# Another first step (ScalarE takes level five, GpSimd part of u, later weight loads), and in the second step scalings and products ahead of weight conversions

## The chip, the cores and the metric

The kernel runs on 1 core of one Trainium2 chip. The metric is device time in microseconds (us). PE is TensorE (PEld its weight loads), DVE is VectorE, ACT is ScalarE, POOL is GpSimd, SP is SyncE, which issues most DMAs. All data are float32; an L and a number is a line of the kernel before.

## The reference, cut to what matters

Two blocks in a row. The first is a recurrence over 768 tokens for 4 x 8 heads of size 48; the second a dense layer with an activation on 3072 tokens.

```python
for t in range(S):                       # per batch and head, state is 48 x 48
    y[t] = r[t] @ (state + outer(u * k[t], v[t]))
    state = w[t][:, None] * state + outer(k[t], v[t])
x = y, with the heads side by side       # 3072 x 384
h = x @ w_in                             # 384 x 2048
out = (h * erf(softplus(h))) @ w_out     # 2048 x 384
```

## The kernel before, in words

The tokens are worked in twelve steps, `s` = 0 to 11, each 128 tokens of two batches. "First step" below is s = 0 (`attend_first`), "second step" is s = 1 (`attend`). The order of the instructions on all five engines is the order in which the program writes them (a manual schedule); each engine works through its own list and waits on semaphores.

**Inside a step.** The recurrence is solved by halving: `own` holds the products of r and k of each pair of tokens in blocks of 64 tokens. It is filled in six levels. At each level PE multiplies r and k (`level_products`, L691) into one of two PSUM banks, DVE multiplies r and k by products of w (`scale`, L357 in the first step by halves, L364 later, the "scalings"), and the result is copied from the bank into `own`: at level 1 by a product with a mask (L947 in the first step, L1087 later), at levels 2 to 5 by DVE's predicated copy with a mask (`take_level`, L701), at level 6 by two ACT copies (L708). The products of w (`tot_sb`) are made by GpSimd (L386 in steps 0 and 1, L438 later). For level 1, r and k with u multiplied in are kept apart in `rk1` (`prepare`, `multiply_u`): in the second step ACT makes both halves (L416, L419). After level 6 PE multiplies `own` by v into the PSUM tile `y` (L723, in two parts), k is transposed (L989 in the first step, L1116 later) and copied to `kT`, the state products follow (L798), a state for the middle of the step is copied out (`middle`), and r times the states is added to `y` (L749). ACT copies `y` out as `y3` and `xT` (L757, L770, L778); in the first step PE does part of that in between ("the hop", L764). `keep_busy` (L1043) and `stay_warm` (L1034) are PE products that nothing reads.

**Beside it, in the second step,** the dense layer of the step before begins: PE multiplies `xT` by w_in (L1206), in six blocks between the levels, two afterwards. w_in and w_out come as 64-bit numbers and are converted on the chip in 16 tiles, two rows of 128 features each: tiles 0 to 7 are w_in, and block n of the products needs tile n. The stages of one tile are named by letters: `l` loads the words (L181; three buffers), `b` scales the high words on ACT (L289), for tiles 0 and 1 into the PSUM tiles `m`, for the others into `y`; `r` scales the low words on ACT (L297) into `rest`; `h` shifts on DVE (L306) from `m` or `y` into the weight; `o` adds `rest` on GpSimd (L319). Since `y` is one tile, the high words of tile n + 1 wait for the shift of tile n, and the products of `own` and v wait for the shift of tile 7.

A load is held back by a small copy into its buffer (L211, L272, L274) from the value that it is to come after; SP issues loads in the written order. `wait_for` (L942) and a copy at L1080 do the same for GpSimd's queue: a one-column copy from the array that DVE's scaling writes, so that what follows on GpSimd comes after it.

In the first step the loads stand as: r, k of the first half, u, r and k of the second half, w, masks (all on SP); tile 0's words; r and k of the second step; v; tile 1's words; w of the second step; tile 2's words; v of the second step. In the second step's loop the shift of the next tile stands ahead of the scaling at levels 3 and up:

```python
if s == 1 and 2 < level:
    stages["h"](level + 1)
scale(s, level)
if s == 1 and level == 2:
    turns.pop("pending")()
if s == 1 and level < 3:
    stages["h"](level + 1)
```

with the addition (`o`) behind it on GpSimd, after the one-column copy of L1080.

Of the kernel before, what the change touches and what calls it, by code (L numbers as in the profile page):

```python
# [23 lines left out]
NJ = 2  # L24
# [67 lines left out]
def kernel(  # L92
# [71 lines left out]
    def products(shape, n=None):  # L164

        if n is None:
            n = turns["next"]
            turns["next"] = 1 - n
        names = "abc"[: len(shape) - 1]
        return banks[n][:].rearrange(  # L170
            f"p ({' '.join(names)}) -> p {' '.join(names)}", **dict(zip(names, shape[1:]))
        )
# [14 lines left out]
    def load_first():  # L187
        t = ins.tile([P, 2, JP, C], FP32, name="in")
        vt = ins.tile([P, NH, D], FP32, name="v")
        ws[0] = ins.tile([P, JP, C], FP32, name="w")  # L190
        n = JP // NJ
        b0, b1 = slice(0, n), slice(n, JP)
        turns["first"] = t5 = t[:].rearrange("p x n t -> p (x n t)").rearrange(
            "p (j x n t) -> p j x n t", j=NJ, x=2, n=NP
        )
        nc.sync.dma_start(out=t5[:, 0], in_=rkw[0][:, 0:2, b0])
        nc.sync.dma_start(out=u_sb[:], in_=u)
        nc.sync.dma_start(out=t5[:, 1, 0], in_=rkw[0][:, 0, b1])
        nc.sync.dma_start(out=t5[:, 1, 1], in_=rkw[0][:, 1, b1])
        nc.sync.dma_start(out=ws[0][:, b0], in_=rkw[0][:, 2, b0])  # L200
        nc.sync.dma_start(out=ws[0][:, b1], in_=rkw[0][:, 2, b1])
        nc.sync.dma_start(out=mask_sb[:], in_=masks)
        loaded[0] = t, vt
# [16 lines left out]
    def load_v(s):  # L220

        vt = loaded[s][1]
        nc.sync.dma_start(out=vt[:], in_=v[s])
# [113 lines left out]
    def rows(e, n=D):  # L337
        return slice(e * EP, e * EP + n)
# [51 lines left out]
    def prepare(s):  # L390


        if s < DIRECT:
            in_t = loaded[s][0]
            rk1 = att.tile([P, 2, JP, C], FP32, name="rk1", bufs=1)
            ready[s] = (rk1,)
            parts = 1 if s else NJ
            def multiply_u(i, x):
                n = slice(i * JP // parts, (i + 1) * JP // parts)
                with_u, plain = (  # L400
                    [
                        t.rearrange("p n (t two) -> p n t two", two=2)[..., one]
                        for t in (rk1[:, x, n], in_t[:, x, n] if s else turns["first"][:, i, x])
                    ]
                    for one in (x, 1 - x)
                )
                if not s and not (x and not i):
                    nc.vector.tensor_mul(
                        with_u[0], with_u[1],
                        u_sb[:, :, None].to_broadcast([P, NP, C // 2]),  # L410
                    )
                    nc.vector.tensor_copy(out=plain[0], in_=plain[1])
                    return
                for p in range(NP):
                    of = slice(p, None, NP)
                    nc.scalar.mul(  # L416
                        out=with_u[0][:, of], in_=with_u[1][:, of], mul=u_sb[:, p : p + 1]
                    )
                nc.scalar.copy(plain[0], plain[1])  # L419

            if s < 2:
                for i in range(parts):
                    for x in range(2):
                        multiply_u(i, x)
                return
            yield
            yield
            multiply_u(0, 0)
# [246 lines left out]
    def first_pair(x, n):  # L675

        return turns["first"][:, n // NP, x, n % NP]
# [19 lines left out]
    def take_level(own, pp, level):  # L697
        half = 1 << (level - 1)
        got = pp[:].rearrange("p e n t -> p (e n) t")
        if level <= MASKED:  # L700
            nc.vector.copy_predicated(  # L701
                rights(own[:], half),
                rights(mask_sb[:, level - 1 : level, :].to_broadcast([P, NH, HC]), half),
                got[..., : HC // 2].rearrange("p n (b h) -> p n b h", h=half),
            )
        else:
            for s0 in range(0, C, HC):
                nc.scalar.copy(own[s0 : s0 + half, :, half:], got[s0 : s0 + half, :, :half])  # L708
# [2 lines left out]

    def from_own(s, own, swap):
        vt = loaded[s][1]
        for j in range(NJ):
            for q in range(0, NP, 2):
                for h in range(NC):
                    e = h ^ swap
                    for p in (q, q + 1):  # L720
                        n = j * NP + p
                        t = slice(h * HC, (h + 1) * HC)
                        nc.tensor.matmul(  # L723
                            y[at(e, p), e, p // 2, j, t],
                            lhsT=vt[t, n * NE + e, :], rhs=own[t, e * JP + n, :],
                            start=swap == 1 and not j and not q, stop=True,
                            skip_group_check=True,
                        )
# [190 lines left out]
    def attend_first(xT):  # L919
# [32 lines left out]
        for level in range(2, LOG):  # L952
            pp = turns.pop("pp", None) or products([P, NE, JP, HC])
            for j, half in enumerate(halves):
                level_products(pp, first_pair, level, half)
                scale(0, level, batch=j)
            turns["pp"] = products([P, NE, JP, HC])
            keep_busy(turns["pp"], (DM,))
            take_level(own, pp, level)
            wait_for(1 << level - 1)  # L960
            if level == 2:
                totals(2, part=slice(batch // 2, batch))
            else:
                totals(*behind[level])
            if level == 2:
                stages["b"](0, 0)
                stages["b"](0, 1)
                stages["r"](0)
                for _ in prepare(1):
                    pass  # L970
                nc.sync.dma_start(out=vt[:], in_=v[0])
                stages["l"](1, own[:, 0, 2:3])
                nc.sync.dma_start(out=ws[1][:], in_=rkw[1][:, 2])
        totals = plan_totals(1)
        pp = turns.pop("pp")
        for j, half in enumerate(halves):
            level_products(pp, first_pair, LOG, half)
            scale(0, LOG, batch=j)
        take_level(own, pp, LOG)

        kT = att.tile([P, NH, D], FP32, name="kT", bufs=1)
        kT_by_e = kT[:].rearrange("p (e n) d -> p e n d", e=NE)
        turned = [products([P, NE, JP, HC])]
        keep_busy(turned[0], (DM,))
        for j, half in enumerate(halves):
            if j:
                turned.append(products([P, NE, JP, HC]))
            for i, n in enumerate(half):
                nc.tensor.transpose(  # L989
                    turned[j][:, 0, 2 * i : 2 * i + 2], first_pair(1, n), ident[:]  # L990
                )
        from_own(0, own, 1)
        for half, ps, copy in zip(halves, turned, (nc.scalar.copy, nc.vector.tensor_copy)):
            copy(
                kT_by_e[:, :, half.start : half.stop],
                ps[:, 0].rearrange("p (n e) d -> p e n d", e=NE)[..., :D],
            )
        stages["b"](1, 0)
        stages["b"](1, 1)
        fence()  # L1000
        stages["l"](2, seen[:, 0:1])
        load_v(1)
        stages["h"](0)
        stages["h"](0)
        ps = [[products([P, NE, JP, HC], 1 - e)[:, e] for e in range(NE)]]
        state_part(0, kT, ps, (0,))
        from_own(0, own, 0)
        nc.scalar.copy(middle[rows(1)], ps[0][1][rows(1), :, :D])
        nc.vector.tensor_copy(middle[rows(0)], ps[0][0][rows(0), :, :D])
        stages["r"](1)  # L1010
        stages["h"](1)
        stages["h"](1)
        wait_for(HC - 1)
        stages["o"](0)
        nc.gpsimd.tensor_mul(faded[1][:], middle[:], ends[:, :, 1:2].to_broadcast([P, JP, D]))
        totals(1)
        stages["o"](1)
        totals(*range(2, LOG + 1))
        through_state(0, xT)

        def pending():
            part = products([P, NE, JP, HC], turns["next"])[:, 0]
# [25 lines left out]
    def attend(s, xT, early, place, behind):  # L1048
# [11 lines left out]
        for level in range(near_log(s) + 1 if s == DIRECT else 1, LOG + 1):  # L1060
# [8 lines left out]
                level_products(pp, rk, level)  # L1069
            if level == LOG and s == DIRECT:  # L1070
                spread_blocks(s + 1, pp)
            if s == 1 and 2 < level:
                stages["h"](level + 1)
            scale(s, level)
            if s == 1 and level == 2:
                turns.pop("pending")()
            if s == 1 and level < 3:
                stages["h"](level + 1)
            if s == 1 and level > 1:
                nc.gpsimd.tensor_copy(out=block_sb[:, 0:1], in_=K[:, 0, 0:1])  # L1080
# [5 lines left out]
            if level == 1:  # L1086
                nc.vector.tensor_mul(  # L1087
                    own[:], got, first[:, None, :].to_broadcast([P, NH, HC])
                )
            else:  # L1090
                take_level(own, pp, level)
            later_on = (s, level) in ((1, 4), (DIRECT, LOG))
            if level > 1 and not later_on:
                next(following, None)
# [687 lines left out]
```

## Time and profile before

| what | value |
|---|---|
| time, median of 3 runs | 573.67 us (573.40 to 574.68) |
| the profiled execution | 573.88 us, its span 572.1 us, granted clock 1.000 |
| busy in the span | PE 563.8 us (99%), PEld 501.2, DVE 452.4, ACT 359.2, POOL 244.6 |
| 0 to 25 us (first step) | PE 22.23, DVE 20.74, ACT 12.57, POOL 9.70; DMA share 0.70 |
| 25 to 51 us (hop and second step) | PE 25.18, DVE 19.53, ACT 17.27, POOL 19.75; DMA share 0.91 |
| 51 to 572 us (the rest) | PE 516.40, DVE 412.09, ACT 329.40, POOL 215.16; DMA share 0.31 |

Busy time is what the profiler recorded between start and end of an instruction. The ends of PE's products are modelled, so a busy PE is not PE at its peak. A line of a timeline has start and length in us, engine, line, operation, what it writes and reads, how often, and in brackets how long its engine stood idle before it and what ended that. A program looks for waits in semaphore events; where several were waited for, it names the last.

### The profile page before, as it was taken

Reading aid. Unit: us, or ns where it says so; the run is one execution under the profiler, and the core shown is the slowest. Engines: PE = TensorE matmul, PEld = TensorE weight load, DVE = VectorE, ACT = ScalarE, POOL = GpSimd, SP = SyncE. Lnnn points to the kernel's source line nnn. Section 1 sums busy time; section 2 is a strip of 40 time slices with the busy share of each in tenths; the row PEclk is TensorE's granted clock in tenths of the full one; section 3 lists DMA queues with packets and bytes.
Section 4 is the critical chain, followed back from the end, with each engine's and each line's share of the span. In section 5 each row is a group of like instructions: output and inputs, shape, how many; then the busy total and the mean of one; then the engine's idle time right before and its main releaser. Section 6 shows DMA issues by size and latency. Waiting matters only on the chain.

```text
span 572.1 us, 16713 instructions
## 1 busy us (share of the span) xinstructions
PE 563.8 (99%) x7320; PEld 501.2 (88%) x7320; DVE 452.4 (79%) x509; ACT 359.2 (63%) x495; POOL 244.6 (43%) x262
## 2 busy tenths in 40 slices
PE   8999999999999999999999999999999999999997
PEld 6688887578998998998998898899899899989997
DVE  7776886999899999699789689689778587477730
ACT  3658877646368867756765766666775771489500
POOL 3567380832884884283575176077073000000000
DMA  8596671440426215245235236335232301000000
GB/s 264 192 315 252 218 230 58 172 158 10 148 69 183 82 63 181 42 147 173 41 123 199 39 111 203 48 112 166 47 111 85 47 9 35 3 2 1 28 29 28
DMA packets 54081, 63.24 MB, mean 111 GB/s; under 512 B 35160, under 2 KB 40568, under 8 KB 52984
## 3 DMA queue, kind: packets, MB, share of 16 engines
q1 hardware_dynamic: 53624, 61.98, 34.4%
q8 instruction: 57, 0.93, 0.7%
q10 hardware_dynamic: 384, 0.20, 0.1%
q14 instruction: 16, 0.13, 0.1%
HBM read 52.39 MB, written 8.69 MB: 107 GB/s over the span
## 4 chain that ended last, share of the span: by engine, by line
PE 75%; DVE 5%; POOL 2%; ACT 1%; issue 1%; ACTq 0%; POOLq 0%
PE m L1328 33%; PE m L1206 27%; PE c L1431 6%; PE pp L691 2%; PE y L723 2%; PE y L749 1%; DVE in L364 1%; PE pp L798 1%; POOL tot_sb L438 1%; POOL w_out_sb L319 1%; PE m L1238 1%; DVE h L1171 1%; PE c L1328 0%; ACTq L784 0%; PE pp L1116 0%
## 5 line engine op out<-in xcount | busy, mean ns | idle before, releaser
L1206 PE MATMUL m<-xT,w_in_sb 128*128 128x256 f32 x960 | 214.5, 381 | 0.2 <-ACT h L1215 0.2
L1206 PEld LDWEIGHTS m<-xT,w_in_sb 128*128 128x128 f32 x960 | 180.1, 190 | 25.2 <-ACT h L1215 0.6
L364 DVE TENSOR_TENSOR in<-in,tot_sb 128x1024 f32<-128x1024 f32 (+1 forms) x55 | 75.7, 1375 | 6.3 <-PE pp L691 5.0
L1215 ACT COPY h<-m 128x512 f32<-128x512 f32 x80 | 46.2, 580 | 51.6 <-PE m L1206 51.3
L1328 PE MATMUL m<-mixed,h 128*128 128x192 f32 x320 | 56.7, 331 | 0.0
L1328 PE MATMUL m<-w_out_sb,h 128*128 128x192 f32 x320 | 56.1, 329 | 0.0
L1328 PEld LDWEIGHTS m<-mixed,h 128*128 128x128 f32 x320 | 51.8, 190 | 0.8
L1328 PEld LDWEIGHTS m<-w_out_sb,h 128*128 128x128 f32 x320 | 52.0, 190 | 0.5
L1328 PE MATMUL m<-w_out_sb,room 128*128 128x192 f32 x288 | 49.7, 326 | 0.0
L1328 PEld LDWEIGHTS m<-w_out_sb,room 128*128 128x128 f32 x288 | 47.3, 190 | 0.1
L493 POOL TENSOR_TENSOR words<-words,own 128x384 f32<-128x384 f32 x21 | 31.2, 1488 | 26.4 <-DVE words L524 13.0
L1166 ACT ACT_TABLE_LOAD x28 | 35.9, 1283 | 8.7 <-DVE h L1171 6.7
L691 PEld LDWEIGHTS pp<-in 48*48 48x48 f32 (+4 forms) x2368 | 30.1, 120 | 11.2 <-issue 5.4
L534 POOL TENSOR_TENSOR words<-words 128x384 f32<-128x384 f32 x28 | 38.7, 1410 | 0.0
L486 POOL TENSOR_TENSOR own<-rest 128x384 f32<-128x384 f32 x7 | 8.5, 1210 | 69.2 <-ACT o L1334 69.2
L1162 ACT ACT_TABLE_LOAD x28 | 35.9, 1283 | 1.8 <-issue 1.3
L691 PE MATMUL pp<-in 48*48 48x32 f32 (+4 forms) x2368 | 33.9, 206 | 0.6 <-DVE in L364 0.6
L438 POOL TENSOR_TENSOR tot_sb<-tot_sb 128x256 f32<-128x256 f32 (+4 forms) x50 | 30.8, 616 | 3.8
L559 DVE TENSOR_REDUCE sums<-rk 128x16 f32<-128x768 f32 (+2 forms) x31 | 31.3, 1022 | 0.0
L1162 ACT ACTIVATE room<-h 128x1024 f32<-128x1024 f32 x28 | 29.6, 1057 | 0.3
L534 POOL TENSOR_TENSOR rk<-words 128x384 f32<-128x384 f32 x28 | 29.6, 1088 | 0.0
L319 POOL TENSOR_TENSOR w_out_sb<-w_out_sb,rest 128x768 int32<-128x768 int32 x8 | 18.7, 2340 | 21.6 <-DVE w_out_sb L311 21.6
(215 smaller groups left out, 1013.2 us busy)
## 6 DMA issues: line engine op xcount, KB each, us to landing
in<-in_rkw SPq DMA_DIRECT2D x8, 1024.0 KB, 5.2
words<-in_moe_w_in SPq DMA_DIRECT2D x16, 384.0 KB, 5.4
words<-in_moe_w_out SPq DMA_DIRECT2D x16, 384.0 KB, 5.9
words<-in_rk_rows SPq DMA_DIRECT2D x8, 768.0 KB, 5.4
w<-in_rkw SPq DMA_DIRECT2D x11, 512.0 KB, 6.8
v<-in_v SPq DMA_DIRECT2D x12, 384.0 KB, 5.7
out<-o SPq DMA_DIRECT2D x23, 192.0 KB, 3.6
in<-in_rkw SPq DMA_DIRECT2D x7, 512.0 KB, 5.8
```

The lines of the kernel that those rows point to most:

```text
L364: nc.vector.tensor_mul(halves, halves, view(tots[level - 1], 0, [[1, n], [2, nb], [0, half]]))
L438: nc.gpsimd.tensor_mul(new, pair[:, :, 0], pair[:, :, 1])
L493: engine.tensor_mul(to, to, of[:, :, None, :].to_broadcast([P, NEAR // 2 // half, half, D]))
L534: engine.tensor_mul(to[:, i], r[:, half:], k[:, part * rows + i, None].to_broadcast([P, half, D]),)
L559: nc.vector.tensor_reduce(out=to, in_=of, axis=mybir.AxisListType.X, op=ALU.add)
L691: nc.tensor.matmul(to, lhsT=rk(1, n)[rows(e), s0 : s0 + m], rhs=right, start=True, stop=True,)
L1162: nc.scalar.activation(sp_room, chunks[0], AF.Softplus)
L1166: nc.scalar.activation(at, sp_room, AF.Erf)
L1206: nc.tensor.matmul(ps[:, ff, :], lhsT=w_in_sb[:, g * FG + f + ff, kk * P : (kk + 1) * P], rhs=xT[:, kk, :], start=kk == 0, stop=kk == KT - 1,)
L1215: nc.scalar.copy(h[:, f : f + FT, :], ps[:])
L1328: nc.tensor.matmul(to, lhsT=a[:, f], rhs=b[:, f], start=start and f == 0, stop=f == FG - 1, skip_group_check=True,)
L1431: nc.tensor.matmul(to[:, f], lhsT=turns["weights"][b][:, i * FT + f], rhs=turns["tokens"][a], start=a + b in STARTS and not f, stop=True, ...
```

## The change

- **Loads at the start:** u is issued on ACT's queue instead of second on SP's.
- **First step, level 5:** instead of DVE's predicated copy, ACT copies the wanted blocks: four copies of 16 partitions x 256 elements (`take_blocks`), ahead of its two copies of level 6.
- **u of the second step:** ACT keeps the first half (`x` = 0). The second half is done by GpSimd, with two products of 128x256 and a copy of 128x512, behind the first step's level 6 (`prepare` is now advanced in two parts by `next(second)`).
- **Later loads:** tile 1's words and w of the second step are issued behind GpSimd's product for level 6 of the first step (before: behind level 2's copy). Tile 2's words and v of the second step come behind `middle` (before: behind the read of `y` called `seen`), held back by an ACT copy instead of one of GpSimd.
- **End of the first step:** all eight transposes of k go into one PSUM bank (before: four into each, after a filler product that is gone). VectorE copies the first half to `kT` and ScalarE the second (before the other way round). The two shifts of tile 0 stand before and after `seen`. ACT's high and low words of tile 1 stand behind the copies of `middle` and `y3` and ahead of `xT` (before: the high words ahead of `middle`, the low words ahead of `y3`). The two shifts of tile 1 follow them on DVE.
- **Second step:** DVE's own-product of level 1 stands ahead of tile 2's shift, and each scaling from level 3 on ahead of the shift of that level's tile (tiles 4 to 7), which it followed.

```diff
@@ load_first
+        nc.scalar.dma_start(out=u_sb[:], in_=u)
         nc.sync.dma_start(out=t5[:, 0], in_=rkw[0][:, 0:2, b0])
-        nc.sync.dma_start(out=u_sb[:], in_=u)
@@ prepare, multiply_u
+                if s == 1 and x:
+                    for j in range(NJ):
+                        of = slice(j * NP, (j + 1) * NP)
+                        nc.gpsimd.tensor_mul(
+                            with_u[0][:, of], with_u[1][:, of],
+                            u_sb[:, :, None].to_broadcast([P, NP, C // 2]),
+                        )
+                    nc.gpsimd.tensor_copy(out=plain[0], in_=plain[1])
+                    return
...
                     for x in range(2):
                         multiply_u(i, x)
+                        yield
@@ new
+    def take_blocks(own, pp, level):
+        half = 1 << (level - 1)
+        got = pp[:].rearrange("p e n t -> p (e n) t")
+        for s0 in range(0, C, HC):
+            for b in range(HC // 2 // half):
+                of = slice(s0 + 2 * b * half, s0 + (2 * b + 1) * half)
+                t = (2 * b + 1) * half
+                nc.scalar.copy(
+                    own[of, :, t : t + half], got[of, :, b * half : (b + 1) * half]
+                )
@@ attend_first
-            take_level(own, pp, level)
+            (take_blocks if level == MASKED else take_level)(own, pp, level)
...
-                for _ in prepare(1):
-                    pass
+                second = prepare(1)
+                next(second)
                 nc.sync.dma_start(out=vt[:], in_=v[0])
-                stages["l"](1, own[:, 0, 2:3])
+            if level == LOG - 2:
+                stages["l"](1, ready[0][1][LOG - 1][:, 0:1])
                 nc.sync.dma_start(out=ws[1][:], in_=rkw[1][:, 2])
...
         take_level(own, pp, LOG)
+        wait_for(HC - 1)
+        next(second)
...
-        turned = [products([P, NE, JP, HC])]
-        keep_busy(turned[0], (DM,))
...
+        turned = products([P, JP, P])
+        turns["next"] = 1 - turns["next"]
+        for n in range(JP):
+            nc.tensor.transpose(turned[:, n, :], first_pair(1, n), ident[:])
         from_own(0, own, 1)
-        for half, ps, copy in zip(halves, turned, (nc.scalar.copy, nc.vector.tensor_copy)):
+        for half, copy in zip(halves, (nc.vector.tensor_copy, nc.scalar.copy)):
...
-        stages["b"](1, 0)
-        stages["b"](1, 1)
+        stages["h"](0)
         fence()
-        stages["l"](2, seen[:, 0:1])
-        load_v(1)
-        stages["h"](0)
         stages["h"](0)
...
+        stages["l"](2, middle[:, 0, 0:1], True)
+        load_v(1)
+        stages["o"](0)
+        nc.gpsimd.tensor_mul(faded[1][:], middle[:], ends[:, :, 1:2].to_broadcast([P, JP, D]))
+        through_state(0, xT)
+        stages["b"](1, 0)
+        stages["b"](1, 1)
         stages["r"](1)
         stages["h"](1)
         stages["h"](1)
-        wait_for(HC - 1)
-        stages["o"](0)
-        nc.gpsimd.tensor_mul(faded[1][:], middle[:], ends[:, :, 1:2].to_broadcast([P, JP, D]))
         totals(1)
         stages["o"](1)
         totals(*range(2, LOG + 1))
-        through_state(0, xT)
@@ attend
-            if s == 1 and 2 < level:
-                stages["h"](level + 1)
             scale(s, level)
...
-            if s == 1 and level < 3:
+            if s == 1 and level > 1:
                 stages["h"](level + 1)
...
+            if s == level == 1:
+                stages["h"](2)
```

## The prediction

> **What bounds the kernel now.** On the page PE is busy 563.8 of the span's 572.1 us; in the windows table it is busy 516.4 of the 521 us after 51 us, where its longest listed wait is 1.10 (113.95, for GpSimd's addition for w_out, work that PE itself had released). So what PE gains or loses by 51 us goes through to the end, and only the first 51 us are worked out. PE's two listed waits in the second step or just ahead of it (engine, line, for whom: us in total, times, longest):
>
> ```profile
> PE pp L691 <- DVE in L364: 0.6, 1, 0.6
> PE y L764 <- ACT y L757: 0.2, 1, 0.2
> ```
>
> PE's timeline (start, length): the first w_in product, the one stall, and the products from `own` that close the second step's levels.
>
> ```profile
> 27.93 2.86 PE L1206 MATMUL m<-xT,w_in_sb 128*128 128x256 f32 x12
> ...
> 39.72 1.03 PE L691 MATMUL pp<-in 48*56 48x32 f32 x64 [0.57 <-DVE in L364]
> ...
> 50.65 0.66 PE L723 MATMUL y<-own,v 64*48 64x64 f32 x32
> ```
>
> Between 27.93 and 50.65 PE works without another stall: an earlier start and the 0.57 are all there is to gain. ScalarE's timeline shows what sets the start, and how little room the end has:
>
> ```profile
> 25.37 0.37 ACT L757 COPY y<-y 128x256 f32<-128x256 f32 x1
> 27.39 0.92 ACT L770 COPY xT<-y 128x256 f32<-128x256 f32 x3 [1.65 <-PE y L764]
> ...
> 42.57 0.89 ACT L289 ACTIVATE y<-words 128x768 f32<-128x768 f32 x1
> ...
> 48.55 1.17 ACT L708 COPY own<-pp 32x512 f32<-32x512 f32 x2
> ```
>
> From 42.57 (high words of w_in tile 6) ScalarE runs without a wait to 49.72, 7.15 us, ending with the copy that L723 needs: 0.93 ahead of it. Last, VectorE's scalings beside GpSimd's work:
>
> ```profile
> 44.88 1.72 DVE L364 TENSOR_TENSOR in<-in,tot_sb 128x1024 f32<-128x1024 f32 x1
> ...
> 48.35 2.81 DVE L364 TENSOR_TENSOR in<-in,tot_sb 128x1024 f32<-128x1024 f32 x1
> ```
>
> ```profile
> 43.68 1.83 POOL L319 TENSOR_TENSOR w_in_sb<-w_in_sb,rest 128x768 int32<-128x768 int32 x1
> 45.47 2.03 POOL L438 TENSOR_TENSOR tot_sb<-w 128x512 f32<-128x512 f32 x1
> ...
> 48.27 1.81 POOL L319 TENSOR_TENSOR w_in_sb<-w_in_sb,rest 128x768 int32<-128x768 int32 x1
> 50.03 1.38 POOL L438 TENSOR_TENSOR tot_sb<-tot_sb 128x128 f32<-128x128 f32 x1
> ```
>
> A scaling takes 1.22 alone. The one at 44.88 ends 1.09 after the addition of 45.51 does; the one at 48.35 ends 1.08 after that of 50.08; and the totals queued behind each (2.03 and 1.38, where the same work takes 1.03 and 0.40 elsewhere) end 0.90 and 0.25 after the scaling. So the two do not overlap: the second waits for the first, then gets its turn ahead of the next. The shift L306 (0.94 at 44.02, inside an addition) is not held up.
>
> The Trainium skill (SBUF — State Buffer, Who interferes with whom) states this as a lock: a VectorE instruction with two SBUF inputs and a GpSimd instruction that reads SBUF exclude each other, whoever issues first. These rows agree. It speaks against this change, which puts every scaling right behind an addition; the sum below goes by the rows, and the rival without that wait is priced beside it.
>
> **First step.** The early DMAs (u on ScalarE's queue, the others 0.5 sooner on SP's) give nothing: PE's warming products run 1.68 to 7.17, its level-1 products to 9.69, and VectorE's 9.84 and 11.47 wait for PE. From there VectorE's order is the same until level 5's predicated copy (0.70) leaves. Level 6's scaling (19.48) then waits for PE's products (first half done at about 19.0, plus 0.2), and for GpSimd's small copy, which now stands there, and its total of 0.22: 19.35, ending 20.65 instead of 20.76. The four ScalarE copies of 16x256 are not in the trace: between 0.31 (one of L770, as many elements) and 0.58 (one of L708) each; I take 0.32, from about 17.9 to 19.2, ahead of the level-6 copies (19.67 before), so hidden; at 0.58 they cost 0.1. PE loses a filler (0.84, L1043) in front of the transposes, hidden by its wait for the scaling. One bank takes all eight transposes; they end at 21.25 (before 21.54). But the built program's waits show both kT copies now in series, ScalarE's behind VectorE's: 21.32 + 0.56, then 0.48 = 22.4. State products start with their second instruction at 22.45, against 22.35: 0.10 late. The `middle` copies follow at 23.6 (ScalarE's was at 23.90, behind high words of tile 1), PE's products with `middle` run 24.29 to 24.78 (before to 24.81). The real gain: y's copy no longer stands behind the low words (0.94): 25.0 to 25.37 instead of 25.37 to 25.74. Then hop 25.45, xT at 27.10 against 27.39. Tile 1's high and low words, moved between y and xT, end at 25.27 + 1.0 + 0.82 = 27.1, just in time. **PE's first w_in product: 27.64, 0.29 earlier.**
>
> GpSimd's share of u: two products of 128x256 and a copy of 128x512. Nearest rows: 0.61 (L386, 128x256) to 1.82 (L1015, broadcast, held up by a scaling) a product; the copy between 0.42 (memset 128x384) and 2.03. I take 0.61 and 0.8, as no scaling runs then: 20.85 to 22.9. Needed by PE at 24.78, so hidden; at the top, 5.7, it is 1.7 late. Addition 0 follows to 24.8 (needed at 27.6).
>
> The later loads: tile 1's words and w issued at about 19.1 instead of 14.57. There, words and w (1.31 MB) were through by 20.2, 5.7 after issue; so 24.8, and the words (first in line) sooner; needed at 25.27. Tile 2's words issue at 24.4 instead of 22.65; with v they were through at 27.3, the words alone at about 26.2 by the 1-us rates: now 27.95, needed at 28.16. Hidden, but with 0.2 to spare.
>
> **Second step.** Scaling 1 and its own-product no longer stand behind a shift; PE's level-2 products still start 2.78 after the first w_in product. Scaling 2 ran 0.53 after these products' end (31.82 to 32.35); elsewhere VectorE follows PE by 0.1. The same instruction has the same waits, so I keep 0.53 (0.1 as the other end, 0.43 sooner): 27.64 + 2.78 + 1.11 + 0.53 = **32.06**. From there the chain runs through the excluded pairs:
> - Additions 2 and 3 start 2.07 later (34.42 - 32.35) and take 3.61 (row at 34.42): 37.74. Scaling 3 is ready at 36.5 and waits: + 1.10 = 38.84. PE wants it at 38.78, so the 0.57 stall shrinks to 0.1.
> - Shift 4 ends 0.88 later (0.96, overlapping 0.08): 39.72. Addition 4 goes at once, 1.82: 41.56; scaling 4 waits for it: 42.66. Shift 5: 43.54, against 42.35 before (41.39 + 0.96).
> - ScalarE's high words of tile 6 use the y bank that shift 5 reads: 43.58, against 42.57. Plus 7.15: its copies into `own` end at 50.73 (49.72). PE, ready at 49.9, now waits; all but its first two products from `own` start at 50.78 and end 0.52 later: 51.30, where they ended at 51.24.
> - Shift 7, now behind scaling 6, must also be done, as these products write the y bank it reads. Scaling 5 ends at 46.48 (43.54 + 0.02 + 1.82 + 1.10); scaling 6 asks 1.41 after that, during a total that ends after 1.55: turn, 1.10, shift: 50.0. In time.
>
> **Sum:** +0.06 us, or -0.37 if scaling 2 follows by 0.1: the 0.29 and the 0.5 of the stall are given back to additions that now go ahead of scalings. 573.88 (profiled execution) becomes 573.5 to 573.9; the median shown is 0.21 below that execution. I predict 573.8.
>
> **Rivals.**
> - No exclusion, or VectorE's turns come first (faster): scaling 3 needs no wait, tile 6's words start at 42.2, PE runs into `own` at 49.83: -0.8, 573.1; with the kT copies side by side (0.35 more), 572.7. For: PE really has that slack. Against: the four rows above. Chance 0.12.
> - Scaling 6 loses its turn (slower): if it asks later than 1.67 after scaling 5's end, where the addition stood before (46.60 to 48.27), that addition goes first: 46.48 + 1.67 + 1.81 + 1.10 + 0.88 = 51.94 for shift 7, PE at 52.08 instead of 50.65: +1.4, 575.3. It decides from 0.26 us; against it, the order of turns in the rows. Chance 0.2.
> - A load is late: words landed 3.4 to 7.1 after issue; 7.1 for tile 1 makes xT 0.9 later, 574.8. Chance 0.06.
> - The change does nothing in step one (start 27.93): 574.2, inside the forecast's case.
>
> The forecast's case has 0.62. A difference of 0.2% is 1.15 us, about what a measurement of this kernel can tell from none: faster 0.1 (the first rival in full), slower 0.24 (the second, and part of the third), same 0.66. Range 572.7 to 575.3.
>
> **What would show it.** xT's copies near 27.1; kT copies in series; scalings 3, 4 and 5 lengthened to over 1.22 with additions right ahead of them; tile 6's high words after 43; PE waiting for ScalarE at the `own` products. Wrong if scalings stay at 1.22, if PE stalls for GpSimd's u, or if ScalarE waits for words before xT.

## The result, and the profile after

| | before | after |
|---|---|---|
| median of 9 runs each | 573.45 us (572.37 to 574.68) | 574.68 us (574.15 to 576.16) |
| profiled execution, its span | 573.88, 572.1 | 574.24, 572.4 |

After over before is 1.0031, 95% interval 1.0018 to 1.0044: slower by 0.3%. The ratio is worked out from all executions; it is not the quotient of the two medians (1.0021 here), and neither are the ratios below. In the second comparison below (e8) it was 1.0039 (1.0026 to 1.0052). The time lies in the forecast's range but on the side of its second rival. In 4 of after's 9 executions the mean granted clock was 0.997 instead of 1.000, and these took 575.78 to 576.16; the other five took 574.15 to 574.68.

Line numbers of after are some 10 to 20 higher than those of before: L1225 is L1206 (w_in), L701 is L691 (level products), L745 is L723 (`own` by v), L718 is L708, L1234 is the copy to `h`.

PE's timeline of after (start, length, then idle before and its releaser): the first w_in product, a new stall, the level where the 0.57 was, and the products from `own`. In the fences, `...` stands where rows are left out.

```profile
26.52 2.86 PE L1225 MATMUL m<-xT,w_in_sb 128*128 128x256 f32 x12
...
35.89 2.83 PE L1225 MATMUL m<-xT,w_in_sb 128*128 128x256 f32 x12 [0.94 <-ACT h L1234]
38.65 1.03 PE L701 MATMUL pp<-in 48*56 48x32 f32 x64
...
51.90 0.66 PE L745 MATMUL y<-own,v 64*48 64x64 f32 x32 [1.95 <-ACT h L1234]
```

PE starts 1.41 earlier (27.93 to 26.52) and is 1.25 late by the products from `own` (50.65 to 51.90). The 0.57 stall is gone, and 1.95 has come. ScalarE of after:

```profile
33.58 0.88 ACT L289 ACTIVATE y<-words 128x768 f32<-128x768 f32 x1 [4.23 <-DMA words<-in_moe_w_in]
...
43.33 0.90 ACT L289 ACTIVATE y<-words 128x768 f32<-128x768 f32 x1 [1.73 <-DVE w_in_sb L306]
...
48.88 0.58 ACT L1234 COPY h<-m 128x512 f32<-128x512 f32 x1
49.35 1.17 ACT L718 COPY own<-pp 32x512 f32<-32x512 f32 x2
```

PE's wait is put down to a copy to `h`; the copies to `h` of this stretch ended at 49.46 and 51.12, and those into `own` at 50.52. None of them can have held PE until 51.90. VectorE's timeline has what did:

```profile
36.50 2.01 DVE L364 TENSOR_TENSOR in<-in,tot_sb 128x1024 f32<-128x1024 f32 x1
...
39.90 2.54 DVE L364 TENSOR_TENSOR in<-in,tot_sb 128x1024 f32<-128x1024 f32 x1
...
43.83 2.53 DVE L364 TENSOR_TENSOR in<-in,tot_sb 128x1024 f32<-128x1024 f32 x1
...
48.11 2.82 DVE L364 TENSOR_TENSOR in<-in,tot_sb 128x1024 f32<-128x1024 f32 x1 [0.25 <-POOL block_sb L1097]
50.85 0.94 DVE L306 TENSOR_SCALAR w_in_sb<-y 128x768 int32<-128x768 int32 x1
```

The last line is shift 7. It ends at 51.79, 0.11 ahead of PE, and it stands behind scaling 6, which took 2.82. GpSimd of after shows why:

```profile
47.89 0.19 POOL L1097 COPY block_sb<-in 128x1 f32<-128x1 f32 x1
48.02 1.82 POOL L319 TENSOR_TENSOR w_in_sb<-w_in_sb,rest 128x768 int32<-128x768 int32 x1
```

The one-column copy reads the array that scaling 6 writes, so the scaling must wait for it (the 0.25), and addition 6 is the very next instruction on GpSimd. When the scaling is released, the addition goes first, by program order and not by luck. The trace before had this pair already, the copy and directly behind it the addition of 48.27:

```profile
48.13 0.18 POOL L1080 COPY block_sb<-in 128x1 f32<-128x1 f32 x1
```

There it cost PE nothing, since shift 7 stood ahead of the scaling.

### The profile page after: what moved, and what is told of

Read it like the earlier page. It is cut to its first block, busy times and chain, and to the rows that moved or that the text cites. A ratio compares the mean times of both kernels' runs of the same rounds, so it can differ in the third digit from the quotient of the medians.

```text
span 572.4 us, 16717 instructions
## 1 busy us (share of the span) xinstructions
PE 562.2 (98%) x7318; PEld 500.7 (87%) x7318; DVE 454.2 (79%) x508; ACT 358.8 (63%) x495; POOL 245.6 (43%) x264
## 4 chain that ended last, share of the span: by engine, by line
PE 82%; DVE 9%; issue 3%; ACT 2%; POOL 2%; DMA 1%; SPq 0%; DVEq 0%; POOLq 0%; ACTq 0%
PE m L1347 33%; PE m L1225 28%; PE c L1450 6%; PE pp L701 4%; DVE in L364 2%; PE y L745 2%; PE m L1257 2%; PE y L771 2%; PE pp L820 1%; PE m L1053 1%; DMA words<-in_moe_w_in 1%; DVE own L711 1%; PE pp L1062 1%; POOL w_out_sb L1288 1%; DVE h L1190 1%
## 5 line engine op out<-in xcount | busy, mean ns | idle before, releaser
L1225 PE MATMUL m<-xT,w_in_sb 128*128 128x256 f32 x960 | 214.4, 382 | 1.2 <-ACT h L1234 1.2
L1225 PEld LDWEIGHTS m<-xT,w_in_sb 128*128 128x128 f32 x960 | 180.4, 190 | 25.9 <-issue 1.3
L364 DVE TENSOR_TENSOR in<-in,tot_sb 128x1024 f32<-128x1024 f32 (+1 forms) x55 | 79.7, 1449 | 6.5 <-PE pp L701 4.4
L1234 ACT COPY h<-m 128x512 f32<-128x512 f32 x80 | 46.2, 579 | 50.3 <-PE m L1225 50.0
L701 PEld LDWEIGHTS pp<-in 48*48 48x48 f32 (+4 forms) x2368 | 30.1, 120 | 11.2 <-issue 6.3
L701 PE MATMUL pp<-in 48*48 48x32 f32 (+4 forms) x2368 | 34.0, 206 | 0.5 <-DVE in L364 0.5
```

What stands on the lines that cost most here:

```text
L364: nc.vector.tensor_mul(halves, halves, view(tots[level - 1], 0, [[1, n], [2, nb], [0, half]]))
L701: nc.tensor.matmul(to, lhsT=rk(1, n)[rows(e), s0 : s0 + m], rhs=right, start=True, stop=True,)
L1225: nc.tensor.matmul(ps[:, ff, :], lhsT=w_in_sb[:, g * FG + f + ff, kk * P : (kk + 1) * P], rhs=xT[:, kk, :], start=kk == 0, stop=kk == KT - 1,)
L1234: nc.scalar.copy(h[:, f : f + FT, :], ps[:])
```

## The experiments

Landmarks of each profiled execution on PE (start of the first step's level-2 products, of the first w_in block, of the products from `own` after the second step's levels), its span, the median, the ratio to the kernel before on the same chip with its interval, and how many executions had a mean clock under 0.998 (the "lower clock" below). Before had 2 of 96 such in the later comparisons, with medians of 572.1 to 572.8; so medians of two rows are compared through their ratios.

| kernel | level 2 | w_in | own | span | median, ratio (interval) | low clock |
|---|---|---|---|---|---|---|
| before | 10.69 | 27.93 | 50.65 | 572.1 | | 2 of 96 |
| after | 9.91 | 26.52 | 51.90 | 572.4 | 574.68, 1.0031 (1.0018-1.0044) | 4 of 9 |
| e1 | 9.79 | 27.09 | 50.16 | 571.2 | 572.92, 1.0001 (0.9990-1.0012) | 1 of 12 |
| e2 | 10.54 | 27.16 | 50.43 | 570.6 | 572.76, 1.0018 (0.9999-1.0036) | 5 of 12 |
| e3 | 10.20 | 29.97 | 54.56 | 575.1 | 576.07, 1.0051 (1.0032-1.0070) | 2 of 6 |
| e4 | 9.99 | 26.61 | 51.19 | 571.5 | 574.79, 1.0037 (1.0021-1.0052) | 2 of 10 |
| e5 | 10.16 | 26.78 | 49.86 | 570.7 | 572.96, 1.0010 (0.9999-1.0021) | 0 of 12 |
| e6 | 9.87 | 26.48 | 49.90 | 570.6 | one run, 572.45 | 0 of 1 |
| e7 | 9.96 | 27.07 | 54.37 | 574.5 | 572.47, 1.0011 (0.9993-1.0029) | 3 of 12 |
| e8 (after) | 10.21 | 27.02 | 51.70 | 572.0 | 574.19, 1.0039 (1.0026-1.0052) | 4 of 12 |
| e9 | 10.64 | 28.73 | 50.84 | 571.2 | 571.99, 0.9982 (0.9968-0.9996) | 0 of 12 |
| e10 | 9.83 | 26.63 | 54.32 | 577.3 | 578.17, 1.0092 (1.0072-1.0111) | 6 of 6 |
| e11 | 9.95 | 26.58 | 49.56 | 569.7 | 572.27, 0.9999 (0.9983-1.0014) | 1 of 12 |
| e12 (e9) | 9.83 | 28.27 | 52.05 | 572.7 | 571.99, 0.9990 (0.9978-1.0001) | 1 of 13 |

**e1_shift7_first.** After, with shift 7 alone back ahead of scaling 6:

```diff
+            if s == 1 and level == LOG:
+                stages["h"](level + 1)
             scale(s, level)
...
-            if s == 1 and level > 1:
+            if s == 1 and 1 < level < LOG:
                 stages["h"](level + 1)
```

> The changed kernel with one thing undone: shift 7 stands ahead of level 6's scaling again. Theory A (the loss is made at the end of the second step: PE's products from own, 51.90 in the changed kernel, wait for shift 7, which waits for scaling 6, which waits for addition 6): these products start with ScalarE's copies, at 50.6 or up to 0.5 earlier, PE's wait of 1.95 there falls to about 0.7, and the time falls by 1.0 to 1.3 us against the changed kernel, to within 0.5 us of the kernel before. Rival B (the loss comes from the later loads, by ScalarE's wait for words of tile 3 and PE's 0.94 behind it): no change, still 1.2 us slower than before. Theory C (a wait of GpSimd's for VectorE near 110 us takes or gives 1.1 whatever comes before): the products start earlier, but PE waits 1 us near 114 again and the time does not move.

VectorE's timeline of e1, then PE's:

```profile
48.39 0.96 DVE L306 TENSOR_SCALAR w_in_sb<-y 128x768 int32<-128x768 int32 x1 [0.35 <-ACT y L289]
49.27 1.85 DVE L364 TENSOR_TENSOR in<-in,tot_sb 128x1024 f32<-128x1024 f32 x1
```

```profile
50.16 0.32 PE L745 MATMUL y<-own,v 64*48 64x64 f32 x4
50.76 0.65 PE L745 MATMUL y<-own,v 64*48 64x64 f32 x28 [0.29 <-ACT own L718]
```

Shift 7 ends at 49.35, the 1.95 is gone, and 0.29 for ScalarE's copies is next, as the forecast had it for the case that shift 7 is in time. The ratio falls from 1.0031 and 1.0039 to 1.0001. One instruction's place is what made after slower. That it is the one-column copy that releases the scaling is read from the profiles; no run moved that copy alone.

**e2_first_step_only** (after's first step, before's order in the second) and **e3_second_step_only** (the reverse).

```diff
+            if s == 1 and 2 < level:
+                stages["h"](level + 1)
             scale(s, level)
...
-            if s == 1 and level > 1:
+            if s == 1 and level < 3:
                 stages["h"](level + 1)
...
-            if s == level == 1:
-                stages["h"](2)
```

> The changed first step alone, with the second step's order of before. Theory A: the 0.6 us that the first step gains reaches the second step; shifts stand ahead of scalings, so only short waits, PE's products from own at 49.9 to 50.4 (50.65 before), time 0.3 to 0.8 us below before. Rival B (loads): ScalarE's wait for words of tile 3 keeps PE's third block at 35.9, the 0.57 stall stays, products from own at 50.3 to 50.7, time equal to before within 0.3. A time of 1 us over before would be against both.

> The second step's new order alone, with the first step of before. Theory A: scaling 6 and shift 7 behind addition 6, products from own at 52.2 to 52.8, PE waiting there 1.5 to 2; time 1.3 to 2 us above before, if nothing is regained later. Rival B: without the later loads no loss; the 0.57 stall gone, time 0.3 to 0.6 below before.

The loss is in the second part: e3 alone is slower by 0.5% (some 3 us, where 1.3 to 2 were expected; 2 of its 6 executions had the lower clock), its scaling 6 again takes 2.83 with the 0.25 for the one-column copy ahead, and its PE waits 1.95 at the products from `own`. (Its profile has 2.50 of other stalls in the first step, told below.) e2 has no such wait; its longest behind the first step is 0.57, for `own`'s product. From its level-2 products to w_in are 16.62 us, as in after (16.61), against 17.24 before. But the 0.3 to 0.8 us that this should have brought did not show (ratio 1.0018), and e2 brought a surprise: 5 of 12 executions at a lower clock, up to 577.0 us. The forecast had nothing for that.

**e4_u_on_sp.** After, with u second on SP's queue again.

> The changed kernel with u back as the second load on SP. In the changed kernel's profile PE's level-1 products start at 6.54 instead of 7.09 and level 2's at 9.91 instead of 10.69. If the earlier loads do that: 7.1 and 10.7 here, time 0.6 to 0.8 us above the changed kernel. If the warming products merely ran at full speed earlier in that one execution (4.84 us for the twelve records instead of 5.49): any start between 6.5 and 7.1, and no difference in time.

Nothing changes: level 2 at 9.99 against 9.91, the wait is 1.94. So the earlier level-2 products of after's profile are not a gain of the early DMAs; what they are is told in the last section.

**e6_no_additions.** The additions (`o`) of tiles 3 to 6 are left out, so these weights lack their low words:

```diff
+            if 3 <= i <= 6:
+                held.pop(i)
             if i in held:
```

> After, but the low words of w_in's tiles 3 to 6 are not added, so that part of the weights' conversion is left out. Theory (the scalings of step two wait for GpSimd's additions, by turns): scalings of levels 3 to 6, which took 2.01, 2.54, 2.53 and 2.82 us, fall to 1.2 to 1.5, shift 7 ends by 50.3, and TensorE's wait of 1.95 ahead of the products from own goes; these start at 50.6 or earlier. Rival (the scalings are long of themselves, as their input comes from TensorE's memory or their shape grows): they stay at 2.0 to 2.8 and the wait at 1.5 or more.

VectorE's timeline of e6, scalings of levels 3 to 6:

```profile
36.91 1.24 DVE L366 TENSOR_TENSOR in<-in,tot_sb 128x1024 f32<-128x1024 f32 x1
...
40.21 1.22 DVE L366 TENSOR_TENSOR in<-in,tot_sb 128x1024 f32<-128x1024 f32 x1 [0.57 <-PE pp L703]
...
43.84 1.23 DVE L366 TENSOR_TENSOR in<-in,tot_sb 128x1024 f32<-128x1024 f32 x1 [0.92 <-PE pp L703]
...
47.30 1.23 DVE L366 TENSOR_TENSOR in<-in,tot_sb 128x1024 f32<-128x1024 f32 x1 [0.71 <-PE pp L703]
```

Without the additions every scaling takes 1.22 to 1.24 instead of 2.01 to 2.82, and PE goes into the products from `own` at 49.90 without a wait. So the long scalings were scalings that waited for an addition.

**e5_loads_after_fence.** e1, with tile 2's words and v asked for where before does:

```diff
         fence()
+        stages["l"](2, seen[:, 0:1])
+        load_v(1)
         stages["h"](0)
...
-        stages["l"](2, middle[:, 0, 0:1], True)
-        load_v(1)
```

> e1_shift7_first with the third tile's words and the second step's v asked for where the kernel before asks for them, behind the fence's copy, instead of behind the copies into middle. In e1 ScalarE idles for the words of the tile behind (in after for 4.23 us, until 33.58) and TensorE then waits 0.59 us at 36.11 for h. Theory (the later loads cost this stall): the words of tile 3 land 0.5 us or more earlier, the wait of TensorE at 36.11 shrinks to under 0.2, products from own start at 49.8 or earlier (50.16 in e1) and the median falls by about 0.3. Rival (the transfers are a full queue, so an earlier request does not land earlier): wait and times stay within 0.2 of e1, median 572.9.

PE's wait for `h` fell from 0.59 to 0.24, and the products from `own` came 0.30 earlier. But counted from the first w_in product they came no earlier (23.08 us against 23.07 in e1), as PE now waited 0.56 for a scaling at 46.28, and the median did not move (both within 0.1% of before). So the theory is not shown. The same wait differs by execution: it is 0.94 in after, 0.23 in e8, 1.37 in e6 and too short to be listed in e4, all with the late requests. None of the five profiles with early requests (before, e3, e5, e9, e12) has more than 0.24 of it; that speaks for the theory, but these kernels differ in more than the requests.

**e7_filler_back.** e2 with the filler product again ahead of the transposes:

```diff
+        keep_busy(products([P, NE, JP, HC], turns["next"]), (DM,))
         turned = products([P, JP, P])
```

> e2_first_step_only with the filler product put back ahead of the transposes. Theory (executions with a mean granted clock of 0.994 to 0.997, 5 of 12 in e2, come from the gap in TensorE's work that the removed filler leaves near 19): no more than 1 of 12 executions is below 0.998, and the transposes start 0.4 us later (20.3 against 19.84), median 572.9 to 573.2. Rival (such executions come by chance, or from elsewhere): again 3 or more of 12.

The theory fell: 3 of 12 executions still had the lower clock, with the filler in place. But the profile fell on one of them (mean 0.994, 576.28 us), and shows where the clock drops. ScalarE, VectorE and PE of e7:

```profile
29.82 0.87 ACT L289 ACTIVATE y<-words 128x768 f32<-128x768 f32 x1 [2.58 <-DMA words<-in_moe_w_in]
```

```profile
30.72 0.96 DVE L306 TENSOR_SCALAR w_in_sb<-y 128x768 int32<-128x768 int32 x1 [3.19 <-ACT y L289]
31.60 1.21 DVE L1107 TENSOR_TENSOR own<-pp,first 128x1024 f32<-128x1024 f32 x1
```

```profile
32.87 1.52 PE L820 MATMUL pp<-v,kT 64*48 64x48 f32 x32 [1.90 <-DVE own L1107]
34.32 5.47 PE L1226 MATMUL m<-xT,w_in_sb 128*128 128x256 f32 x12
```

Tile 2's words landed at 29.8, so ScalarE's high words, VectorE's shift 2 and `own`'s product behind it were late in turn, and PE stood for 1.90. Then a w_in block took 5.47 instead of 2.86. The windows of 1 us have the granted clock at 0.90 from 32 to 33, at 0.50 from 33 to 39 and at 0.68 from 39 to 40: 0.20 + 6.00 + 0.64 = 6.84 us at half speed. In the change as it is, `own`'s product stands ahead of shift 2, and that place of the chain cannot make PE wait.

**e8_after_again.**

> The changed kernel as it is, beside the other three, for the count of executions with a mean granted clock under 0.998 (4 of 9 before) and the gap to the kernel before on one chip. Theory: 574.2 where the clock is 1.0, about 1.7 more where it is 0.997, ratio 1.002 to 1.005. Rival (the first comparison was chance): ratio within 1.001.

The slowdown holds (1.0039), and so does the share at the lower clock: 8 of 21 executions of after in all. In e8 the eight others have a median of 573.93, and the four at 0.997 took 575.64 to 576.17.

**e10_wait_longer.** After, with eight copies of 128 columns ahead of shift 7:

```diff
+            if s == 1 and level == LOG:
+                for _ in range(8):
+                    nc.vector.tensor_copy(
+                        out=spare[:], in_=K[:, 0, :]
+                    )
```

> After with eight short VectorE copies of 128 columns (some 0.2 us each by estimate from the rows) ahead of shift 7, so that TensorE's wait of 1.95 ahead of the products from own grows to some 3.5. Theory (a wait of TensorE of about 2 us brings, in a third of the executions, one stretch of 3.4 us at half clock, some 1.7 us; a longer wait brings it always): nearly all executions show a mean clock of 0.997 or less, the profile shows a granted clock of 0.5 behind 51 us and products there at 2.6 times their length of 0.24, median 574.2 + 1.6 + 1.7 = 577.5. Rival (the lower clock comes by chance and not from this wait): a third of the executions again, median 575.8.

The copies took 2.33, PE's wait grew to 4.30 (the profile calls it "issue", but shift 7 ends at 54.22 and PE starts at 54.32), and all six executions were at 0.994 or 0.997. Windows of e10 of 1 us (window, length, then busy time of PE, PEld, DVE, ACT, POOL, PE's granted clock, DMA share, GB/s):

```profile
52.00:53.00 1.00, 0.00 (x0) 0.00 (x0) 0.86 (x5) 0.00 (x0) 0.34 (x2) 0.84 0.08 31
...
58.00:59.00 1.00, 1.00 (x4) 0.82 (x3) 0.00 (x0) 1.00 (x5) 0.00 (x0) 0.50 0.00 0
59.00:60.00 1.00, 1.00 (x5) 0.86 (x4) 0.00 (x0) 0.98 (x4) 0.00 (x0) 0.75 0.07 16
```

The clock is at half speed from 52.68, 2.7 after PE's last product ended, to 59.5: 0.32 + 6.00 + 0.50 = 6.82 us, 1.6 of it while PE still stood. From the products from `own` to the end this execution takes 523.0, 2.5 more than after's 520.5: about half of the 5.2 us that PE worked at half speed. The median is 5.4 above before's of the same comparison, where e8's is 2.1 above: 3.3 more, of which 2.35 is the longer wait and about 1 is left for the clock. A wait of PE sets the clock back, and a longer wait does it more often.

**e9_early_loads_own_first, e11_own_first_late_loads, e12_e9_again.** The changed first step, `own`'s product of level 1 ahead of shift 2 as in the change, and shifts 4 to 7 ahead of the scalings of levels 3 to 6 as before (shift 3 stands behind scaling 2 in all these kernels); e9 also has e5's early requests. Against after, e11 is:

```diff
+            if s == 1 and 2 < level:
+                stages["h"](level + 1)
             scale(s, level)
...
-            if s == 1 and level > 1:
+            if s == 1 and level == 2:
                 stages["h"](level + 1)
```

> The changed first step, but the third tile's words and v asked for behind the fence's copy as before; in step two own's product stands ahead of shift 2 (as in the change), and shifts 3 to 7 stand ahead of their scalings (as before). Theory (the first step gains 0.6 to 0.8, which the change's second step and late loads give back): no wait of TensorE over 0.3 between 26 and 51 us, products from own at 49.6 to 50.2 by the first step's speed, scalings 3 to 6 at 1.2 to 2.2, at most 1 of 12 executions under a mean clock of 0.998, median 0.3 to 0.8 below the kernel before. Rival (what is won at 50 us is given back in the later steps, at the port or at the end): products from own as early, but a median within 0.2 of before.

> As e9_early_loads_own_first, but with the change's late requests for tile 2's words and v. Theory (in e2 and e7 VectorE's shift 2 waits for ScalarE, which waits for words of tile 2 asked for late, and own's product behind it keeps TensorE waiting 0.6 to 1.9 near 31 us; with own's product first the wait goes): no wait of TensorE for own near 31, at most 1 of 12 executions under a mean clock of 0.998 (8 of 24 in e2 and e7), clean median 572.0 on the scale of e2's. Rival (low clock has another cause): 3 or more of 12.

> The kernel of e9_early_loads_own_first once more, as its first interval (0.9968 to 0.9996) nearly reaches no change. Theory (the first step's gain goes through once no turn is lost and no load is late): ratio 0.997 to 0.999, at most 1 of 12 executions under a mean clock of 0.998, and without a stall for instruction supply the products from own start near 49.9. Rival (the first comparison was luck of the draw): ratio 0.9995 or more.

In e11 PE never waits for `own` near 31 us, although tile 2's words came as late as in e7 (ScalarE's high words at 29.61, after 2.39 of waiting), and 1 of 12 executions has the lower clock. e9 is the fastest kernel: its two comparisons give 0.9982 and 0.9990, of which the first interval ends below 1 and the second just above it. So it beats before by 0.1 to 0.2%, about what can be measured here, and after, itself 0.3 to 0.4% slower than before, by more. Its two profiles missed the landmarks expected of them (`own` at 50.84 and 52.05), as PE stood 1.13 and 1.50 for "issue" in them; of this more in the last section. Counted over e1, e5, e9, e11 and e12, which have no PE wait near 2 us built in, 3 of 61 executions had the lower clock; over after, e3, e4 and e8, which have the 1.95, 12 of 37; over e2 and e7, 8 of 24.

## Why the prediction was wrong, though its range held

The time fell into the range because the range reached as far as the second rival; the forecast's own case, with PE at the products from `own` about where it was, did not happen.

**The step that failed** is "Shift 7, now behind scaling 6, must also be done ... turn, 1.10, shift: 50.0. In time." I priced scaling 6 by the time at which it asks, as if it and addition 6 met by chance, and gave the slower rival 0.2. But the change put the scaling ahead of the shift without moving the one-column copy, and what releases the scaling is that copy, directly ahead of the addition. All five profiles of after's order (after, e3, e4, e8, e10) show the scaling at 2.82 or 2.83 with the addition first. VectorE was free for the scaling at 47.87, 1.51 behind the end of scaling 5, and so inside the 1.67 that the rival allowed; the 0.25 behind that is what lost the turn. The rival's price was near, though by another condition: shift 7 at 51.94 (51.79 measured), PE at 52.08 (51.90), +1.4 (+1.25 at that point).

**The chain up to there** held. Scaling 2 was put 4.42 behind the first w_in product, and is (26.52 to 30.94). Scaling 4 was to end at 42.66 (42.44), shift 5 at 43.54 (43.29), tile 6's high words to start at 43.58 (43.33), ScalarE's copies into `own` to end at 50.73 (50.52). That these agree to 0.3 is in part luck, and so is the rival's price: the chain began 1.12 earlier than forecast (w_in at 26.52 instead of 27.64), and ScalarE's wait for tile 3's words, which the forecast did not have, took 0.8 of that back (addition 3 ended at 37.43, forecast 37.74). Counted from w_in, the rival's PE was 24.44 behind it; measured are 25.38 in after, 24.68 in e8 and 24.58 in e4. The waits for additions 3, 4 and 5 were real (e6). The Trainium skill (SBUF — State Buffer, Who interferes with whom) has this lock, and e6 agrees with it (1.22 to 1.24 without the additions).

**The first step** was right in kind, too small in size. From the level-2 products to w_in, after gains 0.63, where I had 0.29. The term: y's copy, forecast 0.37 earlier, came 0.61 earlier (from the level-2 products 14.68 before, 14.07 after). Most of the 0.24 lies in the state products: I let the copies of `middle` follow 1.15 behind the end of these products' wait for `kT` (22.45 to 23.6), and they followed after 0.96 (21.61 to 22.57). From y's copy to w_in it was 2.54, where I had 2.64, and the transposes ended 0.37 earlier, not 0.29. The rest was as forecast: the early DMAs gave nothing (e4), the kT copies ran in series (PE waits 0.23 for ScalarE's), GpSimd's u was done at 21.8 (1.18 and 0.64, where I took 1.22 and 0.8).

**"Later loads: hidden"** was right for PE in after's profile, where tile 2's words came at 27.6 (forecast 27.95) and ScalarE stood 0.47 for them, but not in general: they came at 28.6 in e2 and 29.8 in e7. And I had not followed tile 3: ScalarE stood 4.23 us for its words (3.73 before) and PE 0.94 for the `h` copy queued behind. How much of that the later request makes stays open (e5).

**"What PE gains or loses by 51 us goes through to the end"** was right, but the profile I started from held 1.10 that no other profile has: PE's wait at 113.95. From the products from `own` to the end, before takes 521.45, after 520.5, and e1 to e6 take 520.2 to 521.0. So the two profiled executions differ by 0.3 only, +1.25 - 0.95, and the medians by 1.23. The +1.25 is net of the 0.78 by which after's level-2 products were early; from these products to `own`, after takes 2.03 longer than before, e8 1.53 and e4 1.24. How often before has that wait in its other executions stays open.

**Not weighed at all: the clock.** With the 1.95, 8 of 21 executions of after ran at 0.997 and took about 2 us longer (575.64 to 576.17 against 573.93 in e8). Averaged, that is some 0.7 of the loss of 0.3 to 0.4%, about 2 us. Neither profile of after fell in such an execution, so that its slow stretch lies behind 51.9 is argued from e10 and from the counts, not seen.

## What to carry to other kernels

When an instruction moves behind one that another engine's work can hold up (here a scaling, held up by an addition), look not for who asks first in the old trace but for the dependence that releases it, and for what stands directly behind that on the other engine. Put the conversions that PE waits for (here shift 7, and `own`'s product) ahead of what can be held up, and a late load or lost turn stays off PE. Price a PE wait near 2 us above its length, and compare the mean clock over many executions, not in one profile.

## What the runs showed of the hardware

**The clock can fall after short waits.** e12's profile has one stretch of its own. PE stood 1.50 for a reason that the profile does not show ("issue"), and the next w_in block took 4.54 instead of 2.86:

```profile
27.89 0.46 PE L701 MATMUL pp<-rk 48*64 48x64 f32 x14 [1.50 <-issue]
28.27 4.54 PE L1227 MATMUL m<-xT,w_in_sb 128*128 128x256 f32 x12
```

Its windows of 2 us (columns as in e10's; the clock is the third number from the end):

```profile
28.00:30.00 2.00, 2.00 (x20) 1.68 (x21) 1.22 (x1) 0.66 (x1) 1.92 (x3) 0.77 0.86 264
30.00:32.00 2.00, 2.00 (x7) 1.56 (x6) 0.96 (x1) 1.03 (x2) 0.98 (x4) 0.50 1.05 392
32.00:34.00 2.00, 2.00 (x81) 1.55 (x81) 0.00 (x0) 1.68 (x3) 0.00 (x0) 0.88 0.97 376
```

That is 0.92 + 2.00 + 0.48 = 3.40 us at half speed, and it begins 1.2 after the wait has ended. e7 and e10 have 6.84 and 6.82, twice as much. The Trainium skill (TensorE: Matmul & The Clock Gate, What's actually happening) states that the clock goes between full and half by a free-running window of 3413 ns: the lengths of these stretches agree. The same page (Why this matters for your kernels) warns of idle gaps over some 3 us; here stretches at half speed followed waits of 1.50 and 1.90, and with a 1.95 in them about a third of the executions had the lower clock, so the measurement decides. It is not a rule for each execution: waits of 1.13 for "issue" in e9, of 1.37 in e6, of 1.92 and 1.95 in e3, and of 1.94 and 1.95 in after, e4 and e8 left the clock at 1.00. That the wait is the cause is argued from the order in three profiles and from the counts.

**The start of the clock is not fixed either.** PE's first twelve warming products took 5.49 in before, 4.84 in after and 4.36 to 5.49 in the experiments. That, not the change, is most of the 0.78 by which after's level-2 products are early; so landmarks are compared from there.

**PE sometimes stands for "issue"** in the middle of a group of equal products, where nothing is waited for: 0.58 and 1.92 in e3, 1.13 in e9, 1.50 in e12, and none of 0.2 or more in before. It comes by execution (e9 and e12 are one kernel with different lengths), and its cause stays open.
